# A mixture-of-experts tail: VectorE tests a unit's size before the last block's scaling, kept weights are signalled at the first piece, and TensorE's jump is prepared earlier in the smallest units

## The chip, the cores and the metric

The kernel runs on one core of a Trainium2 chip. The metric is the device time of one execution in microseconds (us), as the median of several runs. A core has a matrix engine (TensorE, PE in the profile; its weight loads are the row PEld), VectorE (DVE), ScalarE (ACT), GpSimd (POOL), and SyncE (SP), which here issues nearly all DMAs. The engines run their own instruction streams and meet at semaphores.

## The reference

Attention over keys and values that are averaged in groups of eight, and behind it a layer of eight experts, of which each token takes one:

```
k_p, v_p = mean of 8 rows of k, v          # 8 batches, 8 heads, 576 -> 72 keys, head size 64
attn     = softmax(q @ k_p.T / 8) @ v_p
x        = attn as (4608 tokens, 512)
logits   = x @ w_gate                      # 8 experts
e        = argmax(logits);  g = softmax(logits)[e]
out      = g * (relu(x @ w1[e]) @ w2[e])   # w1[e]: 512 x 1024, w2[e]: 1024 x 512, all float32
```

How many tokens an expert gets is known only once the program runs.

## The kernel before, in words

**Stages.** In the first 190 us the attention runs, each token's expert is found, and its row (512 values, gate and token number) is scattered to a list of its expert in device memory (`dispatched`). A short plan then turns the eight counts into a table of *units*. The rest of the span is the expert stage, where the change lies.

**Units.** A unit is up to 512 tokens of one expert. Its size n (table column `K_U`) counts half blocks of 64 tokens, 1 to 8; a block is 128 tokens. Column `K_SW` is 1 when the unit is the first of a new expert, so that its weights have to be brought in, and 0 when the weights are *kept* from the unit before. There are 9 to 16 units (`NUMIN`, `NU`); code exists for all 16, and `more(eng, u, yes, no)` runs `yes` if unit u exists: for u under 9 without a test, from 9 on with a branch on a register. In the profiled execution there are 13 units, with n = 8, 8, 1, 6, 4, 8, 5, 8, 4, 1, 8, 8, 6 by the shapes of the matmuls in the trace (n of 8 gives 512 columns, 6 gives 384, 5 gives 320, 4 gives 256). Units 1, 6, 8, 11 and 12 keep their weights. Units 2 and 9 have one half block.

**Arithmetic.** Each float32 operand is split into a rounded high part and a low part (high made by ScalarE, low by VectorE as the difference), and products are the sum of high x high, high x low and low x high. So before a unit can be computed, its token rows X (transposed by PE or by VectorE) and, at a new expert, its eight weight pieces of 128 x 1024 (0 to 3 for the first layer, signals `A_s1`, `V_s1`; 4 to 7 for the second, `A_s2`, `V_s2`) are split (`whi` by ScalarE, `wlo` by VectorE, `xhi`, `xlo` likewise).

**PE's order in a unit** (`form`). First layer: eight parts f of the hidden layer, one accumulation group each (`mm1`, line 866). ScalarE makes the high part of relu (`hhi`), VectorE the low part (`hlo`, line 1058), which signals `V_h`; part f needs that low part f - 3 is done. With n of 1 the operands are turned round (`mm1_rows`, line 891, in two halves of 512 columns, the result transposed by `ht`, line 902), and VectorE adds the two halves of each column (`hsums`) ahead of `hlo1` (line 1030). Then the next unit's rows may be transposed, and the second layer follows (`product`, line 924): last block first, per k = 0 to 7 two or three products; the first product of part k in the last block waits for low part k and, at every second k, for the weight pieces' signals `A_s2`, `V_s2`. When a block is done PE signals `P_y`.

**Jumps on PE.** The eight sizes have eight bodies, chosen by a `Switch` (`forms`). A `hint` (two register instructions) prepares the jump for the next unit's size. Behind the body follow the last block's high products for k = 2 to 7 (twelve matmuls), common to all sizes, and then the next unit's Switch. The hint stands in the body after block 0's products of k = 0 and 1.

**VectorE's order in a unit** (`dve_unit`). `hidden_lo(u)`: low parts of the hidden layer, and between them the four `wlo` of the second layer's weights, or, if they are kept, one empty instruction (`vnop`, line 799) that adds 4 to `V_s2`. `following`: low parts of the next unit's X and first-layer weights, a chain of branches on that unit's `K_SW` and size. Then the scaling of the blocks by their gates (`y`, line 1284; 1278 to 1282 for a half block), which waits for `P_y` and is followed by GpSimd's scatter to the output (line 1480). Block 0's scaling, `y(0, ...)`, is the last thing of the unit. Then `more` asks whether there is a next unit, and `hidden_lo` tests its size.

The empty signal stands in `hidden`, which VectorE and ScalarE share, after the last of the four parts that carry a weight piece:

```
at = (0, 1, 3, 4) if small else (0, 1, 2, 3) if eng is act else (0, 2, 4, 6)
...
    if u > 0 and f in at:
        with eng.If(entry(eng, K_SW, u, 0, 1) == 1):
            wpart(u, 4 + at.index(f))
        if f == at[-1]:
            with eng.Else():
                nop()
```

**SyncE's order** (`sp_unit`). Rows of unit u + 2 (`xload`, lines 1368 and 1371, and gates, line 1360), then the next expert's second-layer weights (`stage(u, 1)`, line 1403; in a unit of n under 3 only after PE's last product, line 1427), then its first-layer weights (`stage(u + 1, 0)`), each piece once the piece before it in the buffer has been split.

## Time and profile before

| | us |
|---|---|
| median of 3 runs (lowest, highest) | 628.64 (626.46, 629.16) |
| the profiled execution | 629.74 |
| its span in the trace | 628.1 |
| PE busy | 594.5 |
| VectorE busy | 363.3 |
| ScalarE busy | 240.3 |
| GpSimd busy | 169.5 |

The granted TensorE clock is 0.998 of full speed over the span.

A timeline row has the start and the length in us, the engine, the line, the operation, output <- inputs with their shapes, the number of instructions merged into the row, and in brackets how long the engine was idle before it and whose work ended that by the trace's semaphore events. "issue" there means that nothing the trace shows was waited for: the engine's sequencer was busy with registers, branches or fetching. SPq stands for SyncE's own queue. A row of waits has the waiting engine and line, the releaser, the total in us, how often, and the longest.

### The profile page before, as it was taken

What the parts mean: (1) busy time and instruction counts of PE and PEld (TensorE: products, weight loads), DVE (VectorE), ACT (ScalarE), POOL (GpSimd) and SP (SyncE); (2) the same over time, 40 slices, a digit from 0 to 9 for tenths busy, and PEclk for the clock granted to TensorE, in tenths of its full rate; (3) what the DMA queues carried; (4) which work ended last, traced back from release to release, by engine and by line L of the source; (5) the groups of instructions that cost most, each with busy time, mean ns of one, the idle gap of its engine ahead of it and who ended that gap; (6) DMA issues with size and microseconds to landing.
All of it is one profiled execution on the core that took longest, in us unless ns stands there. A gap on an engine that the chain in (4) does not pass through costs nothing.

```text
span 628.1 us, 13333 instructions
## 1 busy us (share of the span) xinstructions
PE 594.5 (95%) x4332; PEld 502.6 (80%) x4332; DVE 363.3 (58%) x736; ACT 240.3 (38%) x445; POOL 169.5 (27%) x250
## 2 busy tenths in 40 slices
PE   6988989999999999989999999999999899999995
PEld 5777978888877888869897889788897678888994
DVE  7698878888871314478588533856145955133220
ACT  2566666786611114065364311423035541021110
POOL 7456655755241220122202011110102311101101
PEclk9999999999999999999999999999999999999999
DMA  8989976994332753619598640064304360100001
GB/s 328 367 229 298 294 204 233 243 271 145 120 135 71 236 170 120 198 48 290 149 267 272 164 139 36 4 211 134 105 35 154 87 184 27 53 0 37 35 4 53
DMA packets 93947, 96.56 MB, mean 154 GB/s; under 512 B 43102, under 2 KB 74846, under 8 KB 93792
## 3 DMA queue, kind: packets, MB, share of 16 engines
q1 hardware_dynamic: 85808, 74.27, 40.7%
q0 software_dynamic: 7440, 20.50, 8.9%
q8 instruction: 61, 1.00, 0.7%
q14 instruction: 94, 0.77, 0.4%
q10 hardware_dynamic: 544, 0.02, 0.0%
HBM read 72.68 MB, written 26.00 MB: 157 GB/s over the span
## 4 chain that ended last, share of the span: by engine, by line
PE 71%; DVE 10%; issue 6%; POOL 4%; SPq 3%; DMA 2%; ACT 2%; DVEq 1%; ACTq 0%; POOLq 0%
PE pU L924 31%; PE pP L866 19%; PE pq L866 9%; PE pU L300 3%; DMA XE<-in_v_dram 2%; PE pP L466 2%; POOL dispatched L409 2%; PE pP L284 2%; PE pq L254 2%; PE pS L264 1%; DVE mx L268 1%; SPq L1368 1%; DVE sd L271 1%; POOL raw L173 1%; DVE raw L173 1%
## 5 line engine op out<-in xcount | busy, mean ns | idle before, releaser
L924 PE MATMUL pU<-W,H 128*128 128x512 f32 x912 | 217.0, 397 | 5.4 <-DVE scr L799 2.8
L924 PEld LDWEIGHTS pU<-W,H 128*128 128x128 f32 x912 | 171.0, 188 | 47.7 <-issue 5.5
L1480 POOL DMA_INDIRECT out_dram<-Y,GT x51 | 54.0, 1060 | 340.3 <-DVE Y L1284 248.5
L866 PE MATMUL pP<-X,W 128*128 128x512 f32 (+3 forms) x660 | 131.5, 353 | 3.3 <-DVEq L1520 1.5
L866 PEld LDWEIGHTS pP<-X,W 128*128 128x128 f32 x660 | 111.6, 188 | 19.9 <-DVEq L1520 1.9
L1037 ACT ACTIVATE H<-pP 128x512 fp32r<-128x512 f32 x56 | 33.4, 597 | 161.5 <-PE pP L866 154.7
L1284 DVE TENSOR_SCALAR Y<-pU,GT 128x512 f32<-128x512 f32 x36 | 26.9, 749 | 104.4 <-PE pU L924 103.2
L1058 DVE SCALAR_TENSOR_TENSOR H<-pP,H 128x512 fp32r<-128x512 f32 (+1 forms) x62 | 39.9, 643 | 64.5 <-ACT H L1037 61.0
L1138 ACT CAST W<-ST 128x1024 fp32r<-128x1024 f32 x56 | 56.9, 1054 | 34.8 <-PE pU L924 24.5
L1146 DVE TENSOR_TENSOR W<-ST,W 128x1024 fp32r<-128x1024 f32 x54 | 64.4, 1217 | 8.0 <-ACT W L1138 5.2
L866 PE MATMUL pq<-X,W 128*128 128x512 f32 (+3 forms) x324 | 67.1, 355 | 0.7 <-ACT W L1138 0.7
L866 PEld LDWEIGHTS pq<-X,W 128*128 128x128 f32 x324 | 55.0, 188 | 9.3 <-issue 1.1
L300 PE MATMUL pU<-V,pt 110*128 110x146 f32 (+3 forms) x468 | 56.7, 282 | 1.4 <-ACT pt L285 0.8
L300 PEld LDWEIGHTS pU<-V,pt 110*128 110x128 f32 (+3 forms) x468 | 51.4, 179 | 3.0 <-ACT pt L285 1.6
L409 POOL DMA_INDIRECT dispatched<-xe,ix x36 | 39.8, 1105 | 18.0 <-POOL ix L370 7.6
L1037 ACT ACTIVATE H<-pq 128x512 fp32r<-128x512 f32 x28 | 16.7, 598 | 71.0 <-PE pq L866 46.9
L1058 DVE SCALAR_TENSOR_TENSOR H<-pq,H 128x512 fp32r<-128x512 f32 (+1 forms) x30 | 19.7, 657 | 27.8 <-ACT H L1037 21.5
L285 ACT COPY pt<-pP 110x384 f32<-110x384 f32 x72 | 30.8, 479 | 6.1 <-PE pP L284 5.7
L268 DVE TENSOR_REDUCE mx<-pS 128x8 f32<-128x576 f32 x36 | 27.1, 752 | 9.6 <-PE pS L264 4.4
L277 ACT ACTIVATE P<-sd 128x576 f32<-128x576 f32 x36 | 24.8, 689 | 18.3 <-DVE sd L271 16.3
L284 PE MATMUL pP<-ident,P 128*110 128x128 f32 x216 | 30.0, 275 | 0.6 <-ACT P L277 0.6
L1116 DVE TENSOR_TENSOR X<-pS,X 128x512 fp32r<-128x512 f32 x34 | 21.9, 683 | 14.7 <-ACT X L1101 10.0
(204 smaller groups left out, 616.5 us busy)
## 6 DMA issues: line engine op xcount, KB each, us to landing
ST<-in_moe_w_dram SPq DMA_DIRECT2D x56, 512.0 KB
raw<-in_k_dram SPq DMA_DIRECT2D x12, 768.0 KB
raw<-in_v_dram SPq DMA_DIRECT2D x11, 768.0 KB
XE<-dispatched SPq DMA_DIRECT2D x104, 64.0 KB, 2.6
qa<-in_q_dram SPq DMA_DIRECT2D x24, 256.0 KB
w<-in_moe_w_dram SPq DMA_DIRECT2D x8, 512.0 KB
XE<-dispatched SPq DMA_DIRECT2D x15, 256.0 KB, 4.1
qa<-in_q_dram SPq DMA_DIRECT2D x2, 1024.0 KB
```

Source lines behind the costliest of these rows:

```text
L268: nc.vector.tensor_reduce(out=mx, in_=s4, axis=AX.X, op=ALU.max)
L284: nc.tensor.transpose(pPs[a][0:R, c * P : (c + 1) * P], Ps[t % 2][:, o : o + R], ident)
L285: take(out=pt[t][a][0:R], in_=pPs[a][0:R, 0 : 3 * P])
L300: nc.tensor.matmul(pu[p0 : p0 + n, a, h * VW : (h + m) * VW], lhsT=pt[t][a][0:r, c % 3 * P + p0 : c % 3 * P + p0 + n], rhs=Vs[g % 2][0:r, ...
L409: apart(nc.gpsimd.indirect_dma_start(out=xs, out_offset=bass.IndirectOffsetOnAxis(ap=at, axis=0), in_=rows, in_offset=None))
L866: r = pe.matmul(out=pH[g % 3][:, :m], lhsT=w1s(w, f, k), rhs=x, start=i == 0, stop=i == len(passes) - 1)
L924: r = pe.matmul(out=pY[:, s % 2, :], lhsT=h, rhs=w[:, k * 512 : (k + 1) * 512], start=start and i == 0, stop=stop and i == len(ps) - 1, sk ...
L1037: act.activation(out=HH[:, f, o], in_=src[:, o], func=AF.Relu).then_inc(Q["A_h"], 1)
L1058: return dve.scalar_tensor_tensor(out=dst[:, f, to], in0=src[:, at], scalar=0.0, in1=f32(HH[:, f, at]), op0=ALU.max, op1=ALU.subtract)
L1138: act.copy(out=(W1H if i < 4 else W2H)[:, o], in_=ST[:, i, :]).then_inc(Q["A_s1" if i < 4 else "A_s2"], 1)
L1146: eng.tensor_tensor(out=(W1L if i < 4 else W2L)[:, o], in0=ST[:, i, :], in1=f32((W1H if i < 4 else W2H)[:, o]), op=ALU.subtract).then_inc( ...
L1480: pool.indirect_dma_start(out=out, out_offset=bass.IndirectOffsetOnAxis(ap=GT[:, u, s, 1:2].bitcast(I32), axis=0), in_=Y[:, s, :], in_offs ...
```

## The change

Three edits, all in the expert stage.

1. **VectorE.** Block 0's scaling moves from the end of a unit to the start of the next, behind the test whether that unit exists and behind a test of n > 1 (`dve_last`, called in both branches). After the last unit it is called by the Else branch of `more`. The code for n = 1 becomes a branch of its own (`hidden_lo1`, `following1`, `alone1`).
2. **Kept weights.** The empty signal comes after the first of the four parts (`at[0]`), on VectorE and on ScalarE, no longer after the last (`at[-1]`).
3. **PE.** In a unit of n = 1 the hint for the next unit stands between the two halves of the first layer; in the others it stays.

```
                     mm1_rows(u, 0)
+                    more(pe, u + 1, lambda: hint(u + 1))
                     mm1_rows(u, 1, range(2))
...
-            more(pe, u + 1, lambda: hint(u + 1))
+            if n > 1 or u == 0:
+                more(pe, u + 1, lambda: hint(u + 1))
...
-                    if f == at[-1]:
+                    if f == at[0]:
                         with eng.Else():
                             nop()
...
+        def hidden_lo1(u):
+            with dve.If(entry(dve, K_SW, u, 0, 1) == 1):
+                wlo(u, 4)
+                wlo(u, 5)
+                hsums(u, 0)
+                wlo(u, 6)
+                hlo1(u, 0)
+                hsums(u, 1)
+                wlo(u, 7)
+            with dve.Else():
+                vnop("V_s2", 4)
+                hsums(u, 0)
+                hlo1(u, 0)
+                hsums(u, 1)
...
+        def dve_last(u):
+            with dve.If(entry(dve, K_U, u, 1, 8) > 1):
+                dve_y(u, 0, False)
+            with dve.Else():
+                dve_y(u, 0, True)
...
+            def following1():
+                go1 = lambda *a: xlo(*a, True)
+                hlo1(u, 1)
+                next_part(dve, u + 1, go1, lambda v: xnone(u + 1, v), wlo, lambda: vnop("V_s1", 4), between=0, first=lambda: None)
+                early()
...
+            def alone1():
+                hlo1(u, 1)
                 early()
...
             n = entry(dve, K_U, u, 1, 8)
             if u > 0:
-                hidden_lo(u)
-            more(dve, u + 1, following, alone)
+                with dve.If(n > 1):
+                    dve_last(u - 1)
+                    hidden_lo(u)
+                    more(dve, u + 1, following, early)
+                with dve.Else():
+                    dve_last(u - 1)
+                    hidden_lo1(u)
+                    more(dve, u + 1, following1, alone1)
+            else:
+                more(dve, u + 1, following, early)
...
-            with dve.If(n > 1):
-                y(0, False)
-            with dve.Else():
-                y(0, True)
...
-        def program(eng, start, unit):
+        def program(eng, start, unit, last=lambda u: None):
             def chain(u):
                 unit(u)
-                if u + 1 < NU:
-                    more(eng, u + 1, lambda: chain(u + 1))
+                more(eng, u + 1, lambda: chain(u + 1), lambda: last(u))
...
-            block.vector(program(dve, dve_start, dve_unit))
+            block.vector(program(dve, dve_start, dve_unit, dve_last))
```

`dve_y` is the body of `y` of before, made a function of the unit.

More of the change, by code (lines that the diff above doesn't have):

```diff
@@ L1202, in hidden_lo @@
             with dve.Else():
-                with dve.If(n > 1):
-                    go(2)
-                with dve.Else():
-                    with dve.If(entry(dve, K_SW, u, 0, 1) == 1):
-                        wlo(u, 4)
-                        wlo(u, 5)
-                        hsums(u, 0)
-                        wlo(u, 6)
-                        hlo1(u, 0)
-                        hsums(u, 1)
-                        wlo(u, 7)
-                    with dve.Else():
-                        vnop("V_s2", 4)
-                        hsums(u, 0)
-                        hlo1(u, 0)
-                        hsums(u, 1)
+                go(2)
+        def hidden_lo1(u):
[12 more added lines that the diff above has]
+                hsums(u, 1)
         def next_part(eng, u, xf, xnop, wf, wnop, turn=None, mid=lambda: None, between=2, first=None):
@@ L1267, in act_unit, with dve_y @@
                 keep(act, u + 2, K_SW, K_U)
-        def dve_unit(u):
-            def y(s, half):
-                dve.wait_ge(Q["P_y"], 4 * u + 4 - s)
-                if u > 0:
-                    dve.wait_ge(sc[s], 16 * u)
-                else:
-                    dve.wait_ge(Q["G_y"], 1)
-                a, gate = pY[:, s % 2, :], GT[:, u, s, 0:1]
-                if half:
-                    dve.tensor_copy(out=Y2, in_=a[64:128])
-                    dve.drain()
-                    dve.tensor_scalar(out=Y2, in0=Y2, scalar1=gate[0:64], scalar2=None, op0=ALU.mult)
-                    dve.drain()
-                    r = dve.scalar_tensor_tensor(out=Y[0:64, s, :], in0=a[0:64], scalar=gate[0:64], in1=Y2, op0=ALU.mult, op1=ALU.add)
-                else:
-                    r = dve.tensor_scalar(out=Y[:, s, :], in0=a, scalar1=gate, scalar2=None, op0=ALU.mult)
-                r.then_inc(Q["V_y"], 1)
+        def dve_y(u, s, half):
+            dve.wait_ge(Q["P_y"], 4 * u + 4 - s)
+            if u > 0:
+                dve.wait_ge(sc[s], 16 * u)
+            else:
+                dve.wait_ge(Q["G_y"], 1)
+            a, gate = pY[:, s % 2, :], GT[:, u, s, 0:1]
+            if half:
+                dve.tensor_copy(out=Y2, in_=a[64:128])
+                dve.drain()
+                dve.tensor_scalar(out=Y2, in0=Y2, scalar1=gate[0:64], scalar2=None, op0=ALU.mult)
+                dve.drain()
+                r = dve.scalar_tensor_tensor(out=Y[0:64, s, :], in0=a[0:64], scalar=gate[0:64], in1=Y2, op0=ALU.mult, op1=ALU.add)
+            else:
+                r = dve.tensor_scalar(out=Y[:, s, :], in0=a, scalar1=gate, scalar2=None, op0=ALU.mult)
+            r.then_inc(Q["V_y"], 1)
+        def dve_last(u):
[3 more added lines that the diff above has]
+                dve_y(u, 0, True)
+        def dve_unit(u):
+            y = lambda s, half: dve_y(u, s, half)
             def following():
@@ L1294, in following @@
                 with dve.Else():
-                    with dve.If(n > 1):
-                        go(small=True)
-                    with dve.Else():
-                        hlo1(u, 1)
-                        go(small=True, first=lambda: None)
-                    early()
-            def alone():
-                if u > 0:
-                    with dve.If(n < 2):
-                        hlo1(u, 1)
+                    go(small=True)
+                    early()
+            def following1():
[5 more added lines that the diff above has]
+                hlo1(u, 1)
                 early()
@@ L1327, in dve_unit @@
             if u > 0:
-                hidden_lo(u)
-            more(dve, u + 1, following, alone)
+                with dve.If(n > 1):
[6 more added lines that the diff above has]
+                    more(dve, u + 1, following1, alone1)
+            else:
+                more(dve, u + 1, following, early)
             if u + 2 < NU:
@@ L1340, in dve_unit @@
                     vnop("V_y", 1)
-            with dve.If(n > 1):
-                y(0, False)
-            with dve.Else():
-                y(0, True)
         def xload(u):
```

## The prediction

> **What bounds the kernel now.** I read the page's list of engines first, then the list of waits for TensorE (PE), then the timeline around each of those waits, and last the chain that ended last. The first row is the share of the span, the others are PE's waits (total us, times, longest).
>
> ```profile
> PE 594.5 (95%) x4332; PEld 502.6 (80%) x4332; DVE 363.3 (58%) x736; ACT 240.3 (38%) x445; POOL 169.5 (27%) x250
> ...
> PE pU L924 <- DVE scr L799: 2.8, 2, 1.6
> PE pU L924 <- DVE H L1030: 2.4, 2, 1.2
> ...
> PE pP L866 <- DVE H L1058: 1.0, 1, 1.0
> ...
> PE pq L866 <- ACT W L1138: 0.7, 1, 0.7
> ...
> PE pP L866 <- DVE W L1146: 0.5, 1, 0.5
> ...
> PE pU L924 <- issue: 0.2, 1, 0.2
> ```
>
> PE is the bound, so only its idle time can be won. In the expert stage the waits that the change can reach are these six rows, 7.6 us together, and L1058's 1.0 is not touched directly: 6.6 us at most. L799 is the empty VectorE (DVE) instruction that signals kept weights; L1030 belongs to the two units of one half block (units 2 and 9). So there are four places: units 6 and 8 (L799), and 2 and 9.
>
> **Kept weights signalled at the first piece.** Unit 6 has n = 5, read from its 320 columns.
>
> ```profile
> 387.38 0.69 DVE L1058 SCALAR_TENSOR_TENSOR H<-pP,H 128x512 fp32r<-128x512 f32 x1 [0.54 <-ACT H L1037]
> ...
> 393.59 3.68 PE L866 MATMUL pP<-X,W 128*128 128x320 f32 x24
> ...
> 397.44 0.67 DVE L1058 SCALAR_TENSOR_TENSOR H<-pP,H 128x512 fp32r<-128x512 f32 x1
> ...
> 398.54 0.15 DVE L799 COPY scr<-scr 128x1 f32<-128x1 f32 x1
> ...
> 398.84 3.52 PE L924 MATMUL pU<-W,H 128*128 128x512 f32 x14 [1.57 <-DVE scr L799]
> 399.49 0.22 DVE L1058 SCALAR_TENSOR_TENSOR H<-pP,H  x1 [0.20 <-issue]
> 400.33 1.29 DVE L1116 TENSOR_TENSOR X<-pS,X 128x512 fp32r<-128x512 f32 x2 [0.62 <-issue]
> ```
>
> PE's first layer ends at 397.27 and its second starts at 398.84, right after the signal at 398.54, which stands behind the seventh low part of the hidden layer (397.44). Signalled at the first part, it is early by six parts. Late next is the low part itself: product k needs part k. Two products at 0.25 us (3.52 over 14) make 0.50 us per k, so k = 6 starts at 400.27 and needs a part that ends before the 398.54 signal; k = 7, at 400.77, needs the one that ends at 399.71. Both are in time, so the whole 1.57 us goes. The empty instruction itself (0.15 us) moves to a place where VectorE waits for ScalarE anyway (0.54 at 387.38): nothing. ScalarE's own signal moves from the fourth piece to the first, and no row waits for it: nothing. Unit 7's low X parts follow at 400.33 and do not hang on PE's products.
>
> Unit 8 (n = 4) has the same wait:
>
> ```profile
> 468.87 1.60 PE L866 MATMUL pq<-X,W 128*128 128x256 f32 x12
> ...
> 471.48 0.12 DVE L799 COPY scr<-scr 128x1 f32<-128x1 f32 x1
> ...
> 471.75 11.48 PE L924 MATMUL pU<-W,H 128*128 128x512 f32 x48 [1.28 <-DVE scr L799]
> ```
>
> 1.28 us on PE by the same reasoning, since three products per k (n = 4) leave the parts more time. In the other kept units (1, 11, 12) no such wait shows: nothing.
>
> **The size test ahead of the last block's scaling.** Today VectorE scales the last block when PE's products land and only then finds out whether there is a next unit and how large it is. At unit 9:
>
> ```profile
> 483.27 0.75 DVE L1284 TENSOR_SCALAR Y<-pU,GT 128x512 f32<-128x512 f32 x1 [4.04 <-PE pU L924]
> 483.33 2.00 ACT L1138 CAST W<-ST 128x1024 fp32r<-128x1024 f32 x2 [7.38 <-PE pU L924]
> ...
> 486.60 2.36 DVE L1146 TENSOR_TENSOR W<-ST,W 128x1024 fp32r<-128x1024 f32 x2 [2.58 <-issue]
> ...
> 491.08 1.20 PE L924 MATMUL pU<-W,H 128*128 128x512 f32 x4 [1.16 <-DVE H L1030]
> ...
> 492.52 3.04 PE L924 MATMUL pU<-W,H 128*128 128x512 f32 x12 [0.23 <-issue]
> ...
> 496.24 3.04 PE L866 MATMUL pq<-X,W 128*128 128x512 f32 x12 [0.69 <-ACT W L1138]
> ```
>
> The first high weights are ready one cast (1.0 us) after 483.33, yet VectorE starts only at 486.60, after 2.58 us of "issue": its jumps. In the changed order they are taken inside the 4.04 us in which it waits for PE. If that cover were gone, the same 2.58 would fall on the scaling and what follows, as today. VectorE gains about 2.2 us, more than PE's 1.16, which goes. Before unit 2 the same edit gives nothing: there ScalarE's cast is last.
>
> ```profile
> 269.86 2.36 DVE L1146 TENSOR_TENSOR W<-ST,W 128x1024 fp32r<-128x1024 f32 x2 [0.39 <-ACT W L1138]
> ...
> 275.07 1.18 PE L924 MATMUL pU<-W,H 128*128 128x512 f32 x4
> ...
> 277.45 3.04 PE L924 MATMUL pU<-W,H 128*128 128x512 f32 x12 [1.20 <-DVE H L1030]
> 277.78 1.29 DVE L1116 TENSOR_TENSOR X<-pS,X 128x512 fp32r<-128x512 f32 x2 [1.15 <-ACT scr L796]
> ...
> 279.58 0.14 DVE L799 COPY scr<-scr 128x1 f32<-128x1 f32 x1
> ...
> 280.98 3.24 PE L866 MATMUL pP<-X,W 128*128 128x384 f32 x17 [0.50 <-DVE W L1146]
> ```
>
> Nothing is moved past a DMA: the scaling issues none, no other queue is touched, and the scatter on GpSimd and PE's wait for the scaling see it at the same time. What the edit adds is code: the scaling stands in both branches, each branch of n > 1 ends in a jump over the other, and after the last unit the scaling stands behind a jump over three units.
>
> **TensorE's jump prepared sooner.** In units 2 and 9 the hint now stands between the two halves of the first layer, no longer behind four products. Two gaps hang on it. At 277.45 PE is idle 1.20 us. The list names VectorE, but products 2 and 3 do not need that instruction; I read it as PE's sequencer handling hint and case exit with only four products queued. At 280.98 it is idle 0.50 us with its data there (the last X signal is at 279.58): the jump, prepared only some 3 us earlier. At its new place the hint stands behind eight queued matmuls; in the wider units, with six or more products queued before and behind it, the list shows no gap that a hint could have made. I take the hint's cost as nothing; its bounds are 0 and the 1.20 seen uncovered.
>
> How much reaches the end at unit 2: the products would end 1.20 sooner, at 280.48 − 1.20 = 279.28, but the X signal ends at 279.72, so unit 3 starts near 279.77: 280.98 − 279.77 = **1.21 us**. Bounds: 1.70 if VectorE's 1.15 us pause before 277.78 shrinks too; a loss of 0.3 if that pause grows to the 2.64 us which the same place shows in unit 3 (1.5 later than now, 281.27):
>
> ```profile
> 302.29 1.29 DVE L1116 TENSOR_TENSOR X<-pS,X 128x512 fp32r<-128x512 f32 x2 [2.64 <-ACT scr L796]
> ```
>
> I take 1.21, since the sequence of tests before that place stays. Unit 3's W2 load waits for PE's last product of unit 2 and moves along.
>
> **Where units 8 and 9 lose theirs.** Their sum is 1.28 + 1.16 + 0.23 + 0.69 = 3.36 us on PE, but unit 10 has a floor that PE does not set:
>
> ```profile
> 476.22 2.35 DVE L1146 TENSOR_TENSOR W<-ST,W 128x1024 fp32r<-128x1024 f32 x2
> ...
> 485.40 10.41 SPq L1368 DMA_DIRECT2D XE<-dispatched  x16
> ...
> 496.46 2.80 SPq L1360 DMA_DIRECT2D GT<-dispatched  x4
> ...
> 502.51 3.37 SPq L1403 DMA_DIRECT2D ST<-in_moe_w_dram  x4
> ...
> 505.73 1.05 ACT L1138 CAST W<-ST 128x1024 fp32r<-128x1024 f32 x1 [5.81 <-DMA ST<-in_moe_w_dram]
> ...
> 508.69 3.66 PE L866 MATMUL pP<-X,W 128*128 128x512 f32 x14 [1.01 <-DVE H L1058]
> 511.43 5.98 SPq L1368 DMA_DIRECT2D XE<-dispatched  x12
> ```
>
> SyncE's queue works from the end of the weights split at 478.57 without a pause that anyone else could end (stage loads, register reads, 16 row loads, 4 gate loads), issues unit 10's W2 at 502.51 (its one wait, for unit 9's last product, has ended at 492.52 + 3.04 = 495.56), and ScalarE, whose next hidden part stands behind that cast, sits 5.81 us. PE waits for it at 508.69. That queue's start hangs on VectorE's work at the end of unit 8, which follows PE's first layer there and not the signal. So PE's 3.36 us turn into wait: 1.01 becomes about 4.4. Contribution: 0 (bounds: 0 and 3.36).
>
> **The end.** The last scaling is behind a new far jump.
>
> ```profile
> 610.59 0.15 DVE L799 COPY scr<-scr 128x1 f32<-128x1 f32 x1 [4.61 <-issue]
> ...
> 621.51 0.75 DVE L1284 TENSOR_SCALAR Y<-pU,GT 128x512 f32<-128x512 f32 x1 [4.86 <-PE pU L924]
> ```
>
> Its cover is 4.86 us; the dearest jump stall of the trace is 4.61. Nothing, with little room.
>
> **The sum**, against the profiled execution (629.74 us, span 628.1, so 1.6 around it): − 1.57 − 1.21 − 0 = − 2.78, 626.96. That execution is 1.1 above the median of 628.64, so against the median **625.9 us**, 0.44% less. A measurement of this kernel tells about 0.5%, 3.1 us, from no change.
>
> **Rivals.**
> *The hint comes too early.* Between hint and jump PE now runs through over thirty matmuls more. If what the hint brought is lost, the jump costs what VectorE's unprepared one did, 2.58, instead of 0.50: unit 3 starts at 279.28 + 2.58 = 281.86, 0.9 late; unit 10's share hides in its wait. − 1.57 + 0.9 = − 0.7: 628.0, so the change hardly does what it says. Against it: in the wide units the hint already outlives 18 products, 4.3 us at 0.24 (11.48 over 48). [...]
>
> *VectorE's longer code stalls in unit 8* (the slower side). Code after unit 1 shifts, and the same place costs 2.64 at 302.29 and next to nothing in unit 8. A stall between unit 8's sixth low part and 476.22 delays SyncE's queue and so unit 10 one for one. It decides from 2.78 us up; at 4.61 the time is 628.64 − 2.78 + 4.61 = 630.5. For it: nothing hides that stretch. Against: most places show none.
>
> *SyncE's floor gives way.* The 16 row loads took 0.65 us each, the 12 at 511.43 took 0.50. At that rate the run is 2.4 us shorter and 2.4 of the 3.36 are kept: − 5.2, 623.4. For it: that pace varies. Against: nothing in the change touches that queue.
>
> **How the numbers follow.** Forecast 0.55 (own range 625.4 to 627.4: unit 2 at 1.70 or − 0.3), hint too early 0.13, VectorE's stall 0.15, floor gives way 0.17. The range takes the last one's 623.4 as its low end and goes up to 629.8, leaving out the worse half of the stall. Faster by over 0.5% means under 625.5: the floor's 0.17 and the low third of the forecast, 0.34. Slower by over 0.5% needs a stall of 4.61 and more besides: 0.07. Between: 0.59.
>
> **What the new profile would show.** Right: no wait of PE for L799; at unit 9 the first weights split about 1 us after ScalarE's cast; PE's gaps in unit 2 gone and unit 3 starting with the X signal; PE's wait for L1058 in unit 10 near 4.4 us. Wrong: a gap of over 1 us before the first matmul of unit 3 with its X signalled, an issue stall of VectorE in unit 8, the last scaling more than 0.1 us after PE's last product, or unit 10's wait still near 1 us.

## The result: 0.5% slower, and the profile after

The changed kernel takes 632.11 us (median of 7 runs, 629.23 to 634.11) against 628.64 us before (7 runs, 626.46 to 630.11): a ratio of 1.0052, 95% interval 1.0034 to 1.0071. The prediction, 625.9 us with a range of 623.4 to 629.8, was wrong in sign. The profiled execution of the changed kernel took 629.23 us (span 627.6, mean granted clock 0.992), the shortest of its seven, so its trace shows rather too little of the loss.

The list of waits after, TensorE's (PE) first and then one row of VectorE's (DVE); columns as before (total us, times, longest):

```profile
PE pU L924 <- issue: 4.9, 2, 2.9
...
PE pS L818 <- DVE Y L1285: 1.6, 1, 1.6
...
PE pU L924 <- DVE H L1032: 1.5, 1, 1.5
...
DVE Y L1285 <- issue: 12.5, 4, 4.3
```

PE no longer waits for L799, as predicted. In its place stands "issue", PE's own sequencer, which had 0.2 us before and has 4.9 now, and a wait for VectorE's scaling (Y) that was not there at all. VectorE itself now stands 12.5 us in "issue" ahead of four scalings. The timeline of the changed kernel at the end of unit 2, and then from unit 8 to unit 10 (start, duration; in brackets the idle time before a group and what ended it):

```profile
276.18 3.04 PE L924 MATMUL pU<-W,H 128*128 128x512 f32 x12 [2.01 <-issue]
...
279.75 4.47 PE L866 MATMUL pP<-X,W 128*128 128x384 f32 x24 [0.53 <-DVE W L1148]
...
466.75 11.41 PE L924 MATMUL pU<-W,H 128*128 128x512 f32 x48
...
472.65 2.35 DVE L1148 TENSOR_TENSOR W<-ST,W 128x1024 fp32r<-128x1024 f32 x2
478.00 2.97 PE L891 MATMUL pP<-W,X 128*128 128x512 f32 x12
478.05 0.75 DVE L1285 TENSOR_SCALAR Y<-pU,GT 128x512 f32<-128x512 f32 x1 [3.05 <-issue]
...
483.06 0.75 DVE L1285 TENSOR_SCALAR Y<-pU,GT 128x512 f32<-128x512 f32 x1 [4.26 <-issue]
483.73 2.35 DVE L1148 TENSOR_TENSOR W<-ST,W 128x1024 fp32r<-128x1024 f32 x2
484.09 1.21 PE L818 MATMUL pS<-ident,XE 128*128 128x128 f32 x8 [1.65 <-DVE Y L1285]
...
488.20 1.20 PE L924 MATMUL pU<-W,H 128*128 128x512 f32 x4 [1.50 <-DVE H L1032]
...
492.25 5.46 PE L924 MATMUL pU<-W,H 128*128 128x512 f32 x12 [2.85 <-issue]
...
497.50 3.07 PE L866 MATMUL pq<-X,W 128*128 128x512 f32 x12
...
498.12 2.59 SPq L1417 DMA_DIRECT2D ST<-in_moe_w_dram  x4
```

Three things are to be seen. Unit 8's second layer (466.75) starts without a wait. VectorE's scaling of unit 8's last block comes at 483.06, 4.9 us after the products it scales ended (466.75 + 11.41 = 478.16); before, it came right behind them (483.27). And in unit 9 PE stands 2.85 us in "issue" in front of the last twelve products, which then take 5.46 us; before, the gap was 0.23 and the twelve took 3.04. The windows of the trace around those twelve give the clock (busy us of each engine with instructions, PEclk the granted clock, DMA share, GB/s):

```profile
488.00:492.00 4.00, 1.20 (x4) 0.67 (x4) 4.00 (x8) 4.00 (x8) 2.78 (x1) 0.86 0.39 90
492.00:496.00 4.00, 3.75 (x9) 3.01 (x10) 4.00 (x6) 1.70 (x2) 0.12 (x1) 0.50 0.08 5
```

The granted clock fell to one half at 490.9, inside the gap and 1.3 us before the products began, and came back at 497.7 when they had ended. So the gap is paid nearly twice: 2.6 us more idle, 2.4 us more for the same twelve products.

The stages, from the starts of PE's rows in the timelines (first product of a stage to first product of the next, us). The five experiments in the table are described below (they ran on two chips, so only lengths are compared); "late" and "early" say where the hint stands in units 2 and 9.

| stage | before | changed | signal alone | signal + test | hint alone | signal, hint late (z2) | signal, hint early (z3) |
|---|---|---|---|---|---|---|---|
| unit 2, second layer to unit 3 | 5.91 | 6.76 | 5.86 | 6.09 | 7.57 | 6.06 | 7.15 |
| unit 6, first layer and wait | 15.81 | 14.08 | 14.08 | 14.08 | 15.81 | 14.08 | 14.08 |
| unit 8, first layer and wait | 12.95 | 11.52 | 11.52 | 11.52 | 12.95 | 11.52 | 11.52 |
| unit 9, first layer and wait | 8.01 | 10.20 | 9.02 | 10.14 | 8.28 | 9.48 | 9.45 |
| unit 9, second layer to unit 10 | 5.16 | 9.30 | 5.38 | 5.15 | 8.31 | 5.38 | 9.16 |
| unit 10, first layer | 23.88 | 22.51 | 22.39 | 22.48 | 22.41 | 22.40 | 22.60 |

The kept signal's gain in units 6 and 8 arrives in full wherever that edit is made (1.73 and 1.43). The loss stands in unit 9's second layer and, smaller, in unit 2's, in each kernel of the table whose hint is early, and in no other of them.

### The profile page after: what moved, and what is told of

The parts are those of the page before. It is cut to its first block, busy times and chain, and to the rows that moved or that the text cites. A ratio compares the mean times of both kernels' runs of the same rounds, so it can differ in the third digit from the quotient of the medians.

```text
span 627.6 us, 13336 instructions
## 1 busy us (share of the span) xinstructions
PE 596.4 (95%) x4332; PEld 505.3 (81%) x4332; DVE 363.5 (58%) x736; ACT 240.5 (38%) x445; POOL 172.5 (27%) x250
## 4 chain that ended last, share of the span: by engine, by line
PE 72%; DVE 11%; issue 6%; POOL 5%; DMA 3%; ACT 1%; SPq 1%; DVEq 1%; POOLq 0%; ACTq 0%
PE pU L924 32%; PE pP L866 20%; PE pq L866 10%; POOL dispatched L409 2%; PE pU L300 2%; DMA XE<-in_v_dram 2%; PE pP L466 2%; DVE mx L268 1%; DVE W L1148 1%; DVE sd L271 1%; PE pP L284 1%; DVE raw L173 1%; POOL raw L173 1%; PE pq L254 1%; PE pq L466 1%
## 5 line engine op out<-in xcount | busy, mean ns | idle before, releaser
L924 PE MATMUL pU<-W,H 128*128 128x512 f32 x912 | 219.2, 400 | 6.4 <-issue 4.9
L1494 POOL DMA_INDIRECT out_dram<-Y,GT x51 | 57.4, 1125 | 342.7 <-DVE Y L1285 253.2
L173 POOL TENSOR_TENSOR raw<-raw 128x768 f32<-128x768 f32 (+1 forms) x18 | 26.4, 1466 | 9.2 <-DMA raw<-in_v_dram 8.5
```

The source lines that it names most:

```text
L173: return lambda: eng.tensor_tensor(out=out, in0=raw[:, :, 0:n], in1=raw[:, :, n : 2 * n], op=ALU.add)
L924: r = pe.matmul(out=pY[:, s % 2, :], lhsT=h, rhs=w[:, k * 512 : (k + 1) * 512], start=start and i == 0, stop=stop and i == len(ps) - 1, sk ...
L1494: pool.indirect_dma_start(out=out, out_offset=bass.IndirectOffsetOnAxis(ap=GT[:, u, s, 1:2].bitcast(I32), axis=0), in_=Y[:, s, :], in_offs ...
```

## The experiments

**Each edit alone, and the change without its third edit.** Four kernels on one chip, five rounds, before at 628.87 us there. Signal alone:

```diff
-                    if f == at[-1]:
+                    if f == at[0]:
```

> Only the second edit: kept weights signalled at the first piece, all else as before. If that edit does what it was meant to and SyncE's row loads set unit 10's pace as in the profile of before, PE's two waits for the empty signal (1.57 us in unit 6, 1.28 in unit 8) go and 1.57 us reach the end: 0.9975 of before. If unit 10's floor is not rigid, unit 8's 1.28 arrives too: 0.9955. If the edit itself is to blame for the changed kernel's loss: over 1.000.

Measured 625.99 us, ratio 0.9961 (0.9948 to 0.9974): faster by 2.5 us. Its timeline has the late hint's gaps, and no wait of PE in unit 10:

```profile
277.98 3.04 PE L924 MATMUL pU<-W,H 128*128 128x512 f32 x12 [1.41 <-issue]
...
474.12 2.35 DVE L1146 TENSOR_TENSOR W<-ST,W 128x1024 fp32r<-128x1024 f32 x2
...
488.51 5.54 PE L924 MATMUL pU<-W,H 128*128 128x512 f32 x16 [2.17 <-DVE H L1030]
...
497.53 2.39 SPq L1403 DMA_DIRECT2D ST<-in_moe_w_dram  x4
...
502.28 2.96 PE L866 MATMUL pq<-X,W 128*128 128x512 f32 x12
505.08 5.76 PE L866 MATMUL pP<-X,W 128*128 128x512 f32 x24
```

Of unit 8's 1.43 us, 1.0 comes back as a longer wait in unit 9 (2.17 for 1.16), and 0.2 because the 16 products there take 5.54 us, part of them at a lower clock (a mean of 0.67 from 488 to 490, 0.50 from 490 to 492).

The size test ahead of the scaling alone (the second part of the diff, the other two left as before):

> Only the first edit: VectorE tests the next unit's size ahead of the last block's scaling. Theory 1 (two jumps instead of one stand before the scaling, and 4 us of cover do not hold them): as in the changed kernel, VectorE idles some 3 us before unit 8's second last scaling and some 4 before its last, which comes 4 to 5 us after PE's last product; PE waits 1 to 2 us for the scaling; unit 9's first low weights come later than before, not sooner; 0 to 1.5 us slower, 1.000 to 1.0025. Rival (the hint alone did the harm, the late scaling was a consequence of its code): scaling within 0.1 us of the product, 1 us faster or nothing, 0.998 to 1.000.

Measured 629.24 us, ratio 1.0007 (0.9988 to 1.0025): nothing to be told. One row of its timeline, in unit 2, is needed below:

```profile
278.11 4.58 PE L924 MATMUL pU<-W,H 128*128 128x512 f32 x12 [1.84 <-issue]
```

The hint alone:

```diff
+                    more(pe, u + 1, lambda: hint(u + 1))
...
-            more(pe, u + 1, lambda: hint(u + 1))
+            if n > 1 or u == 0:
+                more(pe, u + 1, lambda: hint(u + 1))
```

> Only the third edit: the hint of the two small units between the halves of the first layer. Theory 1 (one jump can be prepared at a time, and the early hint displaces the preparation of the jump out of the unit's own body): PE's idle ahead of the twelve common products grows as in the changed kernel, from 1.20 to about 2.0 us in unit 2 and from 0.23 to 2 or more in unit 9, and where the idle time is longest the granted clock drops to half for some 4 us; 1.5 to 4 us slower, 1.0025 to 1.0065. Rival (those gaps came from VectorE's late work): the gaps are as before, 0.998 to 1.000.

Measured 632.79 us, ratio 1.0065 (1.0047 to 1.0082). Its timeline at the end of units 2 and 9:

```profile
277.68 4.58 PE L924 MATMUL pU<-W,H 128*128 128x512 f32 x12 [1.97 <-issue]
282.10 4.40 PE L866 MATMUL pP<-X,W 128*128 128x384 f32 x24
...
493.04 1.19 PE L924 MATMUL pU<-W,H 128*128 128x512 f32 x4 [1.33 <-DVE H L1032]
...
497.09 4.43 PE L924 MATMUL pU<-W,H 128*128 128x512 f32 x12 [2.85 <-issue]
```

The jump into unit 3 (282.10) has no gap left, but not because it is better prepared: the jump itself takes 1.60 us here (1.50 before), and the twelve products, which take 4.58 us for 3.04, cover it. The gap in front of the twelve products grew from 1.20 to 1.97 and from 0.23 to 2.85, and both groups of twelve run slower than 3.04 us.

The change without the hint edit (signal and test):

> The changed kernel without the third edit. Theory 1: gaps ahead of the twelve common products back to 1.2 us or less, full clock through unit 9, VectorE's late scaling stays; 1 to 4 us faster than before, 0.9935 to 0.9985, and 3.5 to 7 us faster than the changed kernel. Rival (VectorE's edit makes the loss): as slow as the changed kernel, 1.003 to 1.006.

Measured 626.57 us, ratio 0.9968 (0.9954 to 0.9981). Its timeline in unit 9:

```profile
485.27 1.20 PE L818 MATMUL pS<-ident,XE 128*128 128x128 f32 x8 [1.59 <-DVE Y L1283]
...
489.37 1.20 PE L924 MATMUL pU<-W,H 128*128 128x512 f32 x4 [1.49 <-DVE H L1030]
490.79 3.05 PE L924 MATMUL pU<-W,H 128*128 128x512 f32 x12 [0.23 <-issue]
```

So PE's new wait for the scaling belongs to the size test where the signal edit is made too (with the test alone PE does not wait for the scaling), and the gap of 2.85 to the hint. Taking the hint edit out of the change makes it 0.84% faster, 5.3 us.

**Is it the hint's place, or that there is a second hint at all?** Each case of PE's switch ends in an exit, a jump to the code that all cases share, and has a hint for it at its start (for its 13 units the changed kernel's trace has 26 branches and 13 hints at the line of the Switch, 984). Theory A: the second hint takes the place of the first, so the exit is no longer prepared. Theory B: the exit costs what it costs, and shows where nothing covers it. Four more kernels, on another chip (before 628.79 us, five rounds). In the first, the signal edit with the hint behind the exit, in the last twelve products, for every unit (the wider ones, which kept their hint, give it twice):

```diff
-            more(pe, u + 1, lambda: hint(u + 1))
+            if n > 1 or u == 0:
+                more(pe, u + 1, lambda: hint(u + 1))
...
+                if k == 2 and u > 0:
+                    more(pe, u + 1, lambda: hint(u + 1))
```

> The second edit alone (x1) with the two small units' hint moved the other way: behind the body's own exit jump, after the first two of the twelve common products (the other sizes give it there a second time). Theory 1 (a hint displaces the preparation of the jump out of the body): nothing displaces it now, so PE's idle ahead of the twelve products falls from 1.2 to 1.4 us in unit 2 to 0.3 or less, and the idle ahead of unit 3 and unit 10 grows, since their jump is prepared some 2.5 us ahead: 0.5 to 1.5 us. Time within 0.3% of x1: 0.993 to 0.998. Rival (the exit jump costs what it costs, and the hint only adds its own instructions): idle ahead of the twelve products stays over 1.0 us in unit 2.

Measured 659.3 us, ratio 1.0469 (1.0443 to 1.0494). In the second, a unit of one half block gives no hint (the first half of the same diff):

> The second edit alone (x1), and the two small units give no hint for the next unit. Theory 1: idle ahead of the twelve common products falls to 0.3 us or less as in y1, while the jump into units 3 and 10 is now wholly unprepared: an idle of 2 to 4 us ahead of their first matmul, and the clock may drop behind it; 0.996 to 1.004. Rival (the exit jump is not prepared by anything): 1.2 us and more ahead of the twelve products as before.

Measured 662.53 us, ratio 1.0533 (1.0505 to 1.0561). Rows of its timeline, at the jumps into units 2 and 3 and in unit 2 between them:

```profile
272.61 2.72 PE L891 MATMUL pP<-W,X 128*128 128x512 f32 x8 [3.68 <-issue]
...
283.78 4.58 PE L924 MATMUL pU<-W,H 128*128 128x512 f32 x12 [1.90 <-issue]
...
293.39 6.44 PE L866 MATMUL pP<-X,W 128*128 128x384 f32 x24 [5.03 <-issue]
```

Two surprises. In both kernels the jumps into all of units 2 to 8 stall, 1.1 to 5.3 us each by the timelines, though units 1 and 3 to 7 are wider and kept their hints. And with no second hint, the exit in unit 2 still shows 1.90 us, so theory A can't be the whole story there.

**VectorE's two jumps.** The change's second edit, with VectorE's branches in the other order (units of one half block first; no hint edit):

```diff
-                with dve.If(n > 1):
+                with dve.If(n < 2):
                     dve_last(u - 1)
-                    hidden_lo(u)
-                    more(dve, u + 1, following, early)
-                with dve.Else():
-                    dve_last(u - 1)
                     hidden_lo1(u)
                     more(dve, u + 1, following1, alone1)
+                with dve.Else():
+                    dve_last(u - 1)
+                    hidden_lo(u)
+                    more(dve, u + 1, following, early)
```

> x4 (first and second edit) with VectorE's two branches in the other order: n = 1 first, wider units in the Else. Theory 1 (the late scaling at the turn from unit 8 to 9 is the sum of two taken jumps, one over the Else at the end of the wide branch, one to the Else of the test): both are gone there, so unit 8's scalings come right behind PE's products, unit 9's first low weights start about 1 us after the product, PE's wait for the scaling (1.6 us) is gone and its wait for unit 9's hidden part falls under 0.5 us. The jumps of 3 to 4 us fall on the wider units instead, where most have 4.9 us of cover, but not behind unit 2, where PE may wait 1 to 2 us for unit 3's hidden part. 0.993 to 0.998. Rival (the stall comes from the length of the code and not from the order): the last scaling of unit 8 still 3 us or more late.

Measured 633.99 us, ratio 1.0077 (1.0051 to 1.0103). From its timeline:

```profile
287.58 0.15 DVE L799 COPY scr<-scr 128x1 f32<-128x1 f32 x1 [5.20 <-issue]
...
290.87 6.03 PE L866 MATMUL pP<-X,W 128*128 128x384 f32 x24 [3.20 <-DVE H L1058]
...
486.58 0.75 DVE L1283 TENSOR_SCALAR Y<-pU,GT 128x512 f32<-128x512 f32 x1 [2.56 <-PE pU L924]
487.72 2.36 DVE L1146 TENSOR_TENSOR W<-ST,W 128x1024 fp32r<-128x1024 f32 x2 [0.39 <-ACT W L1138]
...
492.99 1.18 PE L924 MATMUL pU<-W,H 128*128 128x512 f32 x4
...
496.07 4.59 PE L924 MATMUL pU<-W,H 128*128 128x512 f32 x12 [1.90 <-issue]
```

With the short branch first, the scaling ahead of unit 9 waits for PE alone and the first low weights follow 0.39 us behind the cast, which is what the prediction had expected of the change. The jump over the other branch now falls to the wider units, where it costs more: 5.20 us in unit 3. The last two rows bear on theory B: PE no longer waits ahead of unit 9's four products (492.99), and now the exit behind them costs 1.90 us although the hint is late.

**Is SyncE's queue a floor for unit 10?** Signal alone, with SyncE issuing W2 ahead of the row loads in units of at most two half blocks:

```diff
-                rows()
                 if u > 0:
-                    stage(u, 1)
+                    with sp.If(entry(sp, K_U, u, 1, 8) < 3):
+                        stage(u, 1)
+                        rows()
+                    with sp.Else():
+                        rows()
+                        stage(u, 1)
```

> The second edit alone (x1), and SyncE's order changed: in units of n under 3 the next unit's second-layer weights are issued ahead of the row loads. The forecast held that SyncE's row loads set the start of unit 10's weights and swallow what units 8 and 9 gain. If so, ScalarE's wait for the weights in unit 10 and PE's wait for L1058 there vanish, and up to 2.5 us more than x1 are gained: 0.992 to 0.996. If the floor had already given way in x1 (unit 8's 1.28 us arrived there), no gain over x1: 0.995 to 0.998, and the row loads, now later, may hold up VectorE's transposes in unit 10.

Measured 637.83 us, ratio 1.0126 (1.0097 to 1.0155). What now stands behind came later instead, the row loads and, behind them, the weights of the unit after. The worst place, from the timeline:

```profile
322.83 6.93 SPq L1403 DMA_DIRECT2D ST<-in_moe_w_dram  x8
...
329.70 4.64 PE L866 MATMUL pP<-X,W 128*128 128x256 f32 x24 [8.68 <-DVE H L1058]
```

The low part that PE waits for stands behind a piece of these weights; SyncE loaded them from 307.99 on before, and here only from 322.83.

**The hint's place alone.** Three kernels on a third chip (before 623.99 us there). Five harmless semaphore increments in the place of the hint of a unit of one half block, with the signal edit:

```diff
-            more(pe, u + 1, lambda: hint(u + 1))
+            if n > 1 or u == 0:
+                more(pe, u + 1, lambda: hint(u + 1))
+            else:
+                more(pe, u + 1, lambda: [pe.sem_inc(Q["G_y"], 1) for _ in range(5)])
```

> The signal edit alone, and in a unit of one block TensorE prepares the exit of its body but not the jump to the next unit: five harmless semaphore increments stand where the hint's instructions stood, so that all code lies where it lay in the kernel with the signal edit alone (625.99 us). Theory A (the second hint takes the place of the first, so that the exit is paid): with no second hint the exit is free, the gap before the products of f = 4 and after that follow it in units 2 and 9 is at most 0.3 us, and the jumps into units 3 and 10 cost 2 to 5 us each. Theory B (the exit costs 1.4 to 2 us from the moment TensorE's sequencer comes to it, whatever hints there are): unit 2's gap stays between 1.4 and 2.0 us, unit 9's at nothing behind its wait of about 2 us, and the jumps into units 3 and 10 cost 2 to 5 us. Either gives 629 to 635 us. If the stalls of 1 to 5 us in front of each of units 2 to 8, which two earlier kernels showed, came from the place of the code, they are gone here; if they came from the missing hint, they are here again and the time is near 660 us.

Measured 654.82 us, ratio 1.0476 (1.0432 to 1.0520): the stalls in front of units 2 to 8 are here again. In unit 9 the exit costs next to nothing (a gap of 0.28 us behind the four products); in unit 2 it does not (1.74 and 0.84 us).

The signal edit with the hint four products earlier than before, still behind the whole first layer:

```diff
+            if n == 1 and u > 0:
+                more(pe, u + 1, lambda: hint(u + 1))
...
             for s in range(last, -1, -1):
...
-            more(pe, u + 1, lambda: hint(u + 1))
+            if n > 1 or u == 0:
+                more(pe, u + 1, lambda: hint(u + 1))
```

> The signal edit alone, with the hint of a unit of one block four products earlier than before (ahead of the first four second-layer products rather than behind them), which is still twelve hidden-layer products later than the changed kernel gives it. Theory A: what counts is how long the exit's preparation has run before the second hint replaces it, so the gap behind the exit lies at the late hint's value or between it and the early one's: 1.2 to 2.0 us in unit 2 and 0.2 to 2.8 us in unit 9; a ratio of 0.996 to 1.003. Theory B: as with the late hint, 1.2 to 1.7 us in unit 2 and nothing in unit 9 behind its wait; a ratio of 0.995 to 0.998, and a smaller gap ahead of unit 3.

Measured 622.72 us, ratio 0.9955 (0.9915 to 0.9996). And the signal edit with the changed kernel's early hint (no size test):

> The signal edit and the hint edit without the size test ahead of the scaling. If the effects add (signal alone 0.9961, hint alone 1.0065), the ratio is 1.0026, about 630.3 us, and unit 9 shows an issue gap near 2.9 us and the half clock behind it. If the loss of the full change needs the size test as well (its last scaling was 4.9 us late), the ratio is 0.996 to 0.999. If the signal's gain is lost whenever the hint is early, it is 1.005 or more, as in the full change.

Measured 626.91 us, ratio 1.0034 (1.0001 to 1.0066). These two are the cleanest pair: the same instructions on the same chip, the hint alone in another place. Timeline of the one with the later hint:

```profile
272.52 3.05 PE L924 MATMUL pU<-W,H 128*128 128x512 f32 x12 [1.36 <-issue]
276.05 4.48 PE L866 MATMUL pP<-X,W 128*128 128x384 f32 x24 [0.47 <-issue]
...
485.32 5.54 PE L924 MATMUL pU<-W,H 128*128 128x512 f32 x16 [2.62 <-DVE H L1034]
490.70 2.96 PE L866 MATMUL pq<-X,W 128*128 128x512 f32 x12
```

and of the one with the early hint:

```profile
272.48 4.20 PE L924 MATMUL pU<-W,H 128*128 128x512 f32 x12 [1.97 <-issue]
276.48 4.85 PE L866 MATMUL pP<-X,W 128*128 128x384 f32 x24
...
486.29 2.07 PE L924 MATMUL pU<-W,H 128*128 128x512 f32 x4 [2.49 <-DVE H L1032]
490.19 5.46 PE L924 MATMUL pU<-W,H 128*128 128x512 f32 x12 [1.83 <-issue]
495.45 3.17 PE L866 MATMUL pq<-X,W 128*128 128x512 f32 x12
```

From the first product of unit 9's second layer to unit 10: 490.70 − 485.32 = 5.38 against 495.45 − 486.29 = 9.16, that is 3.78 us. From unit 2's second layer to unit 3: 6.06 against 7.15, 1.09 us. Together 4.9 us, and the two spans, 621.1 and 626.1, differ by 5.0. Nearly nothing else is left to explain.

**The stalls in front of units 2 to 8.** Were they the place of the code, which those kernels also moved? Four tries. The five increments, and the hint behind the exit, each with more room to align TensorE's jump:

```diff
-            pe.addr_align(256, offset=251 if u else 252, max_nops=2)
+            pe.addr_align(256, offset=251 if u else 252, max_nops=64)
```

> The kernel in which a unit of one block prepares no jump (five semaphore increments in the place of the hint), with one number changed: the alignment ahead of TensorE's jump may fill up to 64 slots instead of 2. If the stalls of 1 to 5.5 us in front of units 2 to 8 came from the place of the jump, missed by a few instructions that two fillers could not make good, those in front of units 2 and 4 to 8 are gone, and the ratio is 1.000 to 1.010; if they came from the missing hint, the ratio stays near 1.05. On the exit, free of that disturbance: theory A (the second hint takes the place of the first) has a gap of at most 0.3 us behind the exit in units 2 and 9, theory B (the exit itself costs about 1.5 us) 1.4 to 2.0 us in unit 2. Both: jumps into units 3 and 10 unprepared, 2 to 5 us each.

Measured 661.27 us, ratio 1.0496 (1.0442 to 1.0549).

> The kernel in which a unit of one block gives its hint behind the exit, ahead of its last twelve products, with the same number changed (64 slots instead of 2). If the place of the jump made the earlier form 4.7% slower, this one is near the kernel with the signal edit alone (ratio 0.993 to 0.999); if the late hint did, it stays near 1.047. Theory A: the exit is free, a gap of at most 0.3 us behind it in unit 2, and the jump into unit 3 has 3.0 us of products to be prepared in, so a gap of 0.5 to 2 us there. Theory B: 1.4 to 1.9 us behind the exit in unit 2 as before.

Measured 658.87 us, ratio 1.0464 (1.0404 to 1.0523). Six increments instead of five:

> Six semaphore increments in the place of the hint of a unit of one block, where the earlier kernel had five (654.82 us). The two differ in one instruction, which only units 2 and 9 run. If the place of the code makes the stalls in front of units 2 and 4 to 8 (the hint's first instruction may take two slots once loaded, so that five fillers were one short and six are not), they are gone and the ratio is 1.000 to 1.010, with 2 to 5 us in front of units 3 and 10 and the exit seen alone: theory A at most 0.3 us behind it in unit 2, theory B 1.4 to 2.0 us. If the missing hint makes them, they are here again, near 1.05.

Measured 660.41 us, ratio 1.0502 (1.0322 to 1.0681); behind the exit 0.44 us in unit 9, 1.53 and 1.20 in unit 2. One increment more with the hint kept:

> The kernel with the signal edit alone and one harmless semaphore increment more, ahead of the hint of a unit of one block, so that all later code lies one slot further on. If the place of the code sets whether TensorE's jumps stall, and one slot is enough, the stalls of 1 to 5.5 us in front of units 2 to 8 appear with the hint in place: a ratio of 1.03 to 1.05. If it takes more than one slot, or the missing hint makes them: as with the signal edit alone, 0.994 to 0.998.

Measured 626.97 us, ratio 0.9966 (0.9941 to 0.9992): as without it. Its timeline in unit 9:

```profile
489.60 1.20 PE L924 MATMUL pU<-W,H 128*128 128x512 f32 x4 [2.52 <-DVE H L1032]
491.27 4.57 PE L924 MATMUL pU<-W,H 128*128 128x512 f32 x12 [0.47 <-DVE W L1148]
```

So the alignment of the jump does not do it, and neither does one instruction more. (In the traces a hint is seven instructions of PE's sequencer, not two as said ahead of the prediction, so neither five nor six increments put the code back exactly where it lay.) All six kernels that are some 5% slower lack the hint ahead of the exit in the body of a unit of one half block, and no kernel that has it there shows these stalls. Why a hint in a body that units 1 and 3 to 7 do not run should matter to their jumps stays open. One lead stands in the source and no run tests it. The Switch into unit u is built with `hints[u]`, a name that every body with a hint overwrites, so it gets the hint written last. That is the one of the n = 1 body in the fast kernels, and the one of the n = 2 body or of the shared tail in the six slow ones. Unit 1's jump, which keeps the hint of the n = 1 body, does not stall in them; but the jumps into units 9 to 12 do not either (0.3 to 1.3 us).

## Why the prediction was wrong

**Kept weights signalled at the first piece: right.** 1.57 was forecast for unit 6, and its stage shortened by 1.73; unit 8's 1.28 became 1.43. Alone, this edit is worth 0.39%, near the 0.44% that the whole change was given.

**TensorE's jump prepared sooner: this step failed.** "I take the hint's cost as nothing; its bounds are 0 and the 1.20 seen uncovered", and a gain of 1.21 at unit 2. Measured: the hint edit alone costs 0.65% (4.1 us); added to the signal 0.73% (4.6 us, ratios 0.9961 and 1.0034, on two chips), added to signal and test 0.84% (5.3 us). I read the 1.20 us at 277.45 as the hint being handled together with the exit, so moving the hint would take it away. The exit remained, and the gap grew to about 2 us; in unit 9, where it had been 0.23, it became 1.8 to 2.9 us. The bound of 1.20 was taken from a place where the exit came with the old order, so it bounded nothing in the new one. Nor was the jump better prepared. Exit and jump stand in the traces as branches of PE's sequencer at the line of the Switch. Here are the exit of unit 9 and the jump into unit 3, in the changed kernel and then before (count, shortest/median/longest in ns, first and last start in us):

```profile
L984 PEldq COMPARE_BRANCH  x1: 3878/3878/3878, 488.2 to 488.2; - x1
L984 PEldq COMPARE_BRANCH  x1: 1501/1501/1501, 277.9 to 277.9; - x1
...
L982 PEldq COMPARE_BRANCH  x1: 314/314/314, 492.0 to 492.0; - x1
L982 PEldq COMPARE_BRANCH  x1: 1501/1501/1501, 279.1 to 279.1; - x1
```

The jump into unit 3 takes 1.50 us with the old order and with the new one; over all kernels it takes 1.20 to 1.59 us with the hint late, 1.50 to 1.84 with the hint early, and 2.75 to 4.77 with none ahead of the exit. So giving the hint sooner gained nothing at the jump that it was for.

How the early hint hurts the exit is shown only in part. That its place does it is shown by the pair of the third chip. The exit's own rows say more. With the early hint it takes 3.3 to 3.9 us in both units of one half block, in all three kernels that have it. In unit 9 it starts there only behind PE's wait (1.33 to 2.49 us), which therefore can't cover it. In the other fourteen kernels the exits of units 2 and 9 fall into two groups by the time since the body's own hint for the exit. The thirteen that come over 10 us behind it take 0.31 to 0.44 us (before, unit 9: 0.31 us, 10.1 us behind it); the fifteen that come 9.5 us or less behind it take 1.75 to 3.16 (before, unit 2: 1.84 us, 8.8 us behind it). Unit 2 is always in the second group; unit 9, where PE's wait delays the exit, is in the first, but for the kernel with swapped branches, which has no wait there. So in these runs theory B holds only in this form: a wait helps by what passes before the exit, and not by covering it. It can't explain the early hint in unit 9, whose exits come 10.5 to 12.4 us behind their own hint and take 3.7 to 3.9 us. That fits theory A, that the second hint, 1.0 to 1.2 us behind the first, takes its place; but no run shows the displacement itself. The time alone is no rule for wider units: unit 4's exit takes 1.95 us and more (1.97 before, 2.35 in the changed kernel), and comes over 16 us behind its hint. The gaps behind the exit lie in the exit's own row (3.34 us in unit 2 and 3.88 in unit 9 of the changed kernel). Whether that time goes into fetching, nothing in these runs shows.

My rival "the hint comes too early" had the right culprit at the wrong place. It expected the loss at the jump that the hint is for (0.9 us at unit 3) and none at unit 10; the loss came at the other jump, ahead of it.

**The clock: not in the prediction at all.** Nearly half the loss is TensorE at half clock around such a gap: 5.46 − 3.04 = 2.4 us in unit 9. In the trace of before the clock stays at 1.00 there, so no row warned of it. In these traces it fell to 0.50 around single gaps, of 1.84 us with the test alone (unit 2) and of 2.85 us in the changed kernel (unit 9). In the changed kernel it stayed there for 6.83 us, from 490.92 to 497.75. By the windows of the traces it stayed low for about 3.4 us in unit 9 with the signal alone, in unit 2 with the test alone and in both units with the hint alone, and for 10.2 us in unit 9 with the signal and the early hint.

The length of a gap alone did not decide it. In the changed kernel the gap of 2.01 us in unit 2 left the clock at 1.00, and the twelve products kept their 3.04 us. Behind 2.49 us four products took 2.07 us (signal and early hint), behind 2.52 us four took 1.20 and only the next twelve were slow (signal and one increment). In two traces with more than one fall, the falls lie whole multiples of 3.41 us apart: 133.12 us, 39 times, in the changed kernel (490.92 and 624.04), and 218.5 us, 64 times, with the hint alone (278.3 and 496.8). An estimate from the changed kernel's trace, by its ends of matmuls, which are modelled: counted back from 490.92 in steps of 3.41 us, the last step holds 0.69 us of the gap of 1.50 and 1.52 of the gap of 2.85, together 2.2, and no other step from 200 to 600 us holds more than 1.71 of idle; the gap of 2.01 lies across two steps, 1.71 and 0.30 in them. So what the gaps put into one step may be what counts; no run tests it.

**The size test ahead of the scaling: a step that failed without cost.** "They are taken inside the 4.04 us in which it waits for PE." The cover was shorter, since unit 8's products came sooner by the signal's gain (from the weights split at 475.00 to the products' end at 478.16 is 3.2 us), and there are two stalls, not one: 3.05 ahead of the scaling of the block before the last, 4.26 ahead of the last. The scaling came 4.9 us late and PE waited 1.65 for it. The first low weights were begun 483.73 − 478.16 = 5.6 us behind the products, against 486.60 − 483.23 = 3.4 before. The prediction's own sign of error, "an issue stall of VectorE in unit 8", stood there, though behind the weights (472.65) and not ahead of them, where its rival had put it. By itself the edit measures 1.0007: in its trace the last scaling of unit 8 is 3.2 us late, and PE does not wait for it. PE's wait of 1.6 us came only with the signal, which brings unit 8's products sooner. The swapped branches show that the order of the branches decides who pays.

**SyncE's floor at unit 10: not a floor.** "PE's 3.36 us turn into wait." With the signal alone PE starts unit 10 2.7 us sooner from unit 0 on than before, and does not wait there; unit 10's first layer takes 22.4 to 22.6 us in all six other columns of the table, 23.88 only in the trace of before. From the end of the weights split to the load of W2, SyncE's queue took 23.94 us in the trace of before (478.57 to 502.51), 23.12 in the changed kernel (475.00 to 498.12) and 21.06 with the signal alone (476.47 to 497.53): it varies by more than PE's wait of 1.01. So the gains of units 8 and 9 weren't swallowed at unit 10. Of unit 8's 1.43 us, 1.2 was given back in unit 9 already with the signal alone, and with the early hint far more than that. Here the rival "SyncE's floor gives way" had it right, though the gain that it would have passed on was lost before.

**The end: right.** The last scaling is not late behind its far jump; from the timeline of the changed kernel:

```profile
621.40 0.75 DVE L1285 TENSOR_SCALAR Y<-pU,GT 128x512 f32<-128x512 f32 x1 [4.87 <-PE pU L924]
```

The separate effects, − 0.39%, + 0.07% and + 0.65%, add to + 0.33%; the whole change measures + 0.52%, interval 0.34 to 0.71. The best versions are the signal alone, 0.9961, and the same with the hint four products earlier, 0.9955; the two can't be told apart.

## What to carry to other kernels

When code that prepares one jump is moved, look for the other jump between the new place and the old one: the price showed at the case exit that the hint now ran ahead of, and not at the jump that it was for. A gap bounds the cost of a step only in the order in which it was seen, so a moved step needs a rival that puts the loss at its neighbours. A gap that is gone does not show that its cause is gone: look at the branch's own row, since slower work ahead of it may only cover it. And a gap of 2 us on TensorE was paid twice here in some places, once idle and once at half clock (with the hint alone in unit 2, 1.97 us and 1.54 more for the same twelve products), and once in others (2.01 us in the changed kernel's unit 2); look at the granted clock around each new gap.

## What the runs showed of the hardware

- In the units of one half block a case exit took PE's sequencer 3.3 to 3.9 us when the next unit's hint was given 1.0 to 1.2 us behind the exit's own (six exits in three kernels; 3.34 and 3.88 in the changed kernel). In the other fourteen kernels it took 0.31 to 0.44 us in the thirteen cases in which it came over 10 us behind its own hint, and 1.75 to 3.16 us in the fifteen in which it came within 9.5 us.
- The jump into unit 3 took 1.20 to 1.84 us with a hint ahead of the exit (1.50 both before and in the changed kernel), and 2.75 to 4.77 us without one.
- The granted clock fell to 0.50 around single gaps of PE, of 1.84 us (test alone, unit 2) and 2.85 us (changed kernel, unit 9), and stayed low for about 3.4 us (signal, test or hint alone), 6.83 us (changed kernel) or 10.2 us (signal and early hint); twelve products of 3.04 us then took 4.2 to 5.5. One gap of 2.01 us (changed kernel, unit 2) left it at 1.00.
- VectorE's jumps left it idle for 3.05 and 4.26 us in the changed kernel, one after the other, where no wait covered them (1.2 us of the first are register reads behind the jump), and for 5.20 us with the branches swapped.
- Without the hint in the body of a unit of one half block, or with one in the shared tail, the jumps into seven units stalled 1.0 to 5.5 us each, and the kernels were some 30 us slower (654.8 to 662.5 us); aligning the jump did not change it (661.27 and 658.87 us).
